# First FFN: later stores of converted chunks and a later first fetch of expert weights; the joint stage's opening in another order

## The chip, the core and the metric

The kernel runs on one core of a Trainium2 chip. The metric is device time in microseconds (us), the median of a few runs of the whole program. The core has a matrix engine (TensorE, PE in the profile), a vector engine (VectorE, DVE), an activation engine (ScalarE, ACT), a general engine (GpSimd, POOL) and a queue engine (SyncE, SP) that here only issues transfers. Each engine takes its instructions strictly in program order: one that waits holds up all that stand behind it on the same engine.

## The reference, cut to what matters

```python
x = attention(q, k, v, n_global, n_local)           # 1536 tokens x 512, 8 heads, local window
h = x @ w_in                                        # first FFN: 512 -> 2048
g = h * np.tanh(softplus(h))
x = g @ w_out                                       # 2048 -> 512
p = domain_probs / (domain_probs.sum(-1, keepdims=True) + 1e-09)
for e in range(4):                                  # second layer: 4 experts, 512 -> 1024 -> 512
    h = np.maximum(x @ w1[e], 0.0)
    out += p[:, e:e + 1] * (h @ w2[e])
```

`attention` and `softplus` stand for code that is left out here. `w_in` and `w_out` arrive as 64-bit floats and are made into 32-bit ones on the chip.

## The kernel before, in words

The 1536 tokens are three blocks of 512. The order of work is: attention of block 0, then the first FFN of block 0 (with the attention of blocks 1 and 2 mixed in at its end), the experts on block 0 (all but the last chunk of weights), the first FFN of blocks 1 and 2, and then a joint stage, in which the experts run on blocks 1 and 2 together. No scheduler reorders anything: each engine's queue is what the code issues, line after line.

**First FFN of block 0** (`first_block`). Its weights come in 16 chunks of 1 MB (64-bit). Four buffers, `big0`, `big1`, `raw0`, `raw1`, take them in turn, so the fetch of chunk c can start only when chunk c-4 has been converted. The string `PLAN` is the order of issue, a letter for each step, counted up as it occurs:

- `a`: ScalarE begins the conversion of a chunk (L602, one instruction, reads the fetched buffer); `t`, three for a chunk: VectorE ends it (L605, L607, L609). The result is the tile `w0`, `w1`, ... in a ring of buffers. After the third `t` of chunk c, `ahead()` issues the fetch that its buffer is free for (L581). In the kernel before, the converted chunk is stored to DRAM (`wfirst`, L613, 512 KB) by the third `t` too, ahead of that fetch. The stores are read again only by the first FFN of block 1.
- `H`: the first product of a chunk, 4 matmuls in plain fp32, which the trace counts as 8 records; `P`: the second product, as long.
- `e`, `c`, `n`, `l`, `u`, `v`, `g`: the gate function between them. `e`, `n`, `l` are ScalarE's (L663, L671, L676 and L677), `c`, `u`, `v`, `g` VectorE's (L667, L682, L686, L690). `g` gives the tile that `P` multiplies.
- `w`: a part of the first expert chunks' split (L629, L632), whose weights `w16`, `w17`, `w18` are fetched in `hidden` (L586) when s reaches a number.

In this stage chunk 4 is, for example, `h4`, `e4`, `n4` and, after `g`, the operand of the fifth `P`.

**The joint stage** (`late_block`) opens with 13 groups of products before it comes to a steady order. `hidden(q, m)` is product m of pair q of expert chunks (L892, 6 matmuls of 128x512): a left operand (`in`, the weights, or `sums`, sums of them) and a right one (`y1`, `y2`, `t2`, `t3`, `t4`: rows of blocks 1 and 2 or their differences), each split into a high and a low half (names that end in h and l). Products 1, 6, 7 and 4 of a pair add up in one PSUM bank (`ha0` for pair 0, `ha1` for pair 1); 2, 5 and 3 use another (`hx0`, `hx1`), each of them starting it anew. Between two of a bank, ScalarE or VectorE has to read the bank (L899, L903): these are the drains. The operands `y2`, `t2`, `t3`, `t4` are made in the generator `combine_rows` from the last FFN's result: subtractions and casts on VectorE and ScalarE, part of them between the products, at each `next(self.combining)`. `project(0)` and `project(1)` (L735, 12 matmuls each) end the FFN of block 2 and the last expert chunk of block 0; the latter is followed by `add_expert`, four VectorE instructions (L796) and the store of the result. `late_part(1, "sums")` is a cast on ScalarE (L873, to `sumsh1`) and two subtractions on GpSimd (L875, to `sumsl1`). `late_project` is L937.

Of the kernel before, what the change touches and what calls it, by code (L numbers as in the profile page):

```python
# [1 line left out]

# [38 lines left out]

PLAN = (
    "SSYXXESYSEXSEDXNXESNTDCTXSENAZNEXATTSCZEDAXANSFSNEXTTDCNEZAXANTETSCZaADXNAtSFNTEXSCTXEAZSEDAVSVaXTTX"
    "CSEZAEADVVFTXTCEZAAaDVVTtTCaAZtAFtHttttHetactntlHteauvgHcetntltaPuavgcetPntltauHvgctntlPteauvgHctntl"
    "tPeuavgctnPtltauvHgtttPecattnltHuvgatPtectnltHtauvgHetcattnHlteuvgPcetntltHwuvgctnPtltieuvHgcwnwlPeu"
    "vgcnljHwjuvgwP12ecnlwHuvg34612Pecnl3uvg5Hw4w6w12Pecnl3uvg54P6Q"
)

# [490 lines left out]
class Body:  # L539
# [48 lines left out]
    def narrow(self, s):  # L588

        if s not in self.w64:
            return
        nc, raw = self.nc, self.w64.pop(s)
        word = raw.bitcast(I32).rearrange("p (n t) -> p n t", t=2)
        top = raw.bitcast(F32).rearrange("p (n t) -> p n t", t=2)[:, :, 1]
        if self.first:

            m = self.w32[s] = self.ring.tile([P, 1024], F32, tag="wl" if s % 2 else "wh", name=f"w{s}")
        else:  # L600
            m = self.w32[s] = self.wpool.tile([P, 1024], F32, tag="w", name=f"w{s}")
        nc.scalar.activation(m, top, AF.Abs, scale=TO_F32)  # L602
        yield
        mi = m.bitcast(I32)
        nc.vector.tensor_scalar(mi, mi, 0x0FFFFFFF, 3, ALU.bitwise_and, ALU.logical_shift_left)  # L605
        yield
        nc.vector.scalar_tensor_tensor(mi, word[:, :, 1], -0x40000000, mi, ALU.bitwise_and, ALU.bitwise_or)  # L607
        yield
        nc.vector.scalar_tensor_tensor(mi, word[:, :, 0], 29, mi, ALU.logical_shift_right, ALU.bitwise_or)  # L609
        if self.first:  # L610

            yield
            nc.sync.dma_start(self.wfirst[s], m)  # L613

    def part(self, s):

# [101 lines left out]
    def project(self, *steps):  # L718

        nc, (kind, t, n) = self.nc, self.steps[steps[0]]  # L720
        opens, closes = steps[0] in self.opens, steps[-1] in self.closes
        if opens:
            acc = [self.acc_ps.tile([P, 512], F32, tag=f"acc{d}", name=f"acc{steps[0]}_{d}") for d in range(4)]
            self.acc = [(d, a, slice(0, 512)) for d, a in enumerate(acc)]
        chunks = [(self.ws.pop(s), self.g.pop(s)) for s in steps]
        for d, acc, h in self.acc:
            for k, ((wh, wl), (gh, gl)) in enumerate(chunks):
                if kind == "ffn":
                    c = slice(512 + d * P, 512 + (d + 1) * P)
                    mms = (wh[:, c], gh), (wl[:, c], gh), (wh[:, c], gl)  # L730
                else:
                    c, w = slice(d * P, (d + 1) * P), slice(512 + h.start, 512 + h.stop)
                    mms = (gh[:, c], wh[:, w]), (gh[:, c], wl[:, w]), (gl[:, c], wh[:, w])
                for m, (a, r) in enumerate(mms):
                    nc.tensor.matmul(acc[:, h], a, r, start=opens and k == 0 and m == 0,  # L735
                                     stop=closes and k == len(chunks) - 1 and m == 2)
            if closes and kind == "moe":
                e = n // NF2
                self.add_expert(t, e, d, acc, h, n == 0 or self.closes[steps[-1]] == 0, self.closes[steps[-1]] == 1)
        if closes and kind == "ffn":  # L740
            self.end_ffn(t)

# [59 lines left out]
    def combine_rows(self):  # L802
# [28 lines left out]
            nc.vector.tensor_tensor(t[2][:, k, :], acc[2 + k], t[1][:, k, :], ALU.subtract)  # L831
        for k in range(2):
            nc.scalar.copy(t[0][:, k, :], acc[2 + k])
        lo(1)
        hi(2)
        yield
        lo(2)
        nc.vector.tensor_tensor(t[3], t[0], t[3], ALU.subtract)
        yield
        hi(3)  # L840
        nc.vector.tensor_tensor(t[4], t[4], t[2], ALU.subtract)
        lo(3)
        hi(0)
        lo(0, nc.gpsimd)
        yield
        hi(4)
        lo(4)
        yield


# [25 lines left out]
        self.wp[q, what] = hi, lo  # L876


    def late_hidden(self, q, m):


        nc = self.nc
        bank, opens, what, at = PRODUCTS[m]
        if opens and m in (1, 2):
            self.hb[q, bank] = self.bank(f"h{bank}{q}")
        ps = self.hb[q, bank]
        (wh, wl), (rh, rl) = self.wp[q, what], self.rows[m]
        n = 0
        for kc in range(2):
            c = slice(at * 256 + kc * P, at * 256 + (kc + 1) * P)  # L890
            for a, r in ((wh, rh), (wl, rh), (wh, rl)):
                nc.tensor.matmul(ps, a[:, c], r[:, kc, :], start=opens and n == 0, stop=n == 5, skip_group_check=True)  # L892
                n += 1
        self.flush()
        if m == 1:
            self.hs[q] = [self.temps[(3 * q + k) % len(self.temps)] for k in range(3)]
        t = self.hs[q]
        if m in (1, 6, 7):
            nc.scalar.copy(t[(1, 6, 7).index(m)], ps)  # L899
        if m in (2, 7, 3):  # L900
            k = {2: 0, 7: 2, 3: 1}[m]
            b = self.hb[q, "x"]
            nc.vector.tensor_tensor(t[k], b, t[k], ALU.add)  # L903
            self.late_relu(q, {2: (0, 0), 7: (1, 1), 3: (1, 0)}[m], t[k])
        if m == 4:
            self.late_relu(q, (0, 1), ps)
# [49 lines left out]
    def late_block(self, project):  # L956


        n, order = NE * NF2 // 2, (1, 2, 6, 5, 7, 4, 3)
        hidden = self.late_hidden  # L960
        hidden(0, 1)
        project(0)
        hidden(0, 2)
        hidden(1, 1)
        next(self.combining)
        hidden(0, 5)
        hidden(0, 6)
        next(self.combining)
        project(1)
        next(self.combining)  # L970
        hidden(0, 7)
        hidden(1, 2)
        self.late_part(1, "sums")
        self.late_weights(1, "out")
        self.late_weights(2, "in")
        hidden(0, 4)
        hidden(0, 3)
        for q in range(1, n + 1):
            tasks = {}
            if q < n:  # L980
# [5 lines left out]
                    tasks[9] = lambda: self.late_part(q + 1, "sums")  # L986
                if q + 2 < n:
                    tasks[8] = lambda: self.late_weights(q + 2, "in")
            left = [m for m in order if q < n and (q > 1 or m > 2)]
            for k in range(8):  # L990
                if k < len(left):
                    hidden(q, left[k])
# [15 lines left out]
    def first_block(self, ready, now):  # L1008
# [46 lines left out]
            return run  # L1055

        def hidden(s):
            if s == 4:
                for c in range(NF1, NF1 + 3):
                    self.fetch(c)  # L1060
            assert n["F"] == 4 and n["t"] >= 3 * s + 3
            self.accumulating = True
            self.hidden_first(s)
            ahead()

        def project(s):
            self.project_first(s)
# [9 lines left out]
        def convert(k):  # L1077
# [1 line left out]
            assert n["a"] > c  # L1079
            next(narrowing[c], None)  # L1080
            ahead()
            if k % 3 == 2:
                next(narrowing[c], None)

        def part(k):
            c, third = divmod(k, 3)
# [35 lines left out]
    def run(self):  # L1122
# [14 lines left out]
                self.closes[s] = 0 if n == NF2 - 1 and kind == "moe" else 1 if s == last - 1 else 2  # L1137
        self.x, self.y, self.outs, self.nr, self.yf, self.rows = {}, {}, {}, {}, {}, {}
        self.w64, self.w32, self.ws, self.h, self.enr, self.g = {}, {}, {}, {}, {}, {}
        self.w2, self.wp, self.late = {}, {}, None  # L1140
        bias = self.bias.rearrange("p h c -> p (h c)")
        self.sums, self.rest = [bias[:, 0:1024], bias[:, 1024:2048]], bias[:, 2048:3072]
        ready = dict(fetch=0, narrow=0, part=0)
# [166 lines left out]
```

## Time and profile before

| | us |
|---|---|
| median of 3 runs | 892.99 (892.88 to 895.15) |
| profiled execution | 892.84 |
| its span | 891.0 |
| TensorE busy in the span | 873.6 (98%), 3848 instructions |
| VectorE, ScalarE, GpSimd busy | 566.5 (64%), 481.8 (54%), 385.9 (43%) |
| granted clock over the span | 0.997 |

A row of a timeline gives the start, the duration, the engine, the line and the tiles of an instruction or of a run of like ones, and in brackets how long the engine had been idle before it and what it waited for. Matmuls are pipelined: the duration of one reaches into the next, so the time that a group costs is read from start to start. A window's row gives, for each engine, its busy time in that stretch and its number of instructions, then the clock that TensorE was granted, the busy share of the 16 DMA engines and their rate.

### The profile page before, as it was taken

The page shows a single profiled execution, that of the slowest core. Times are in us where ns is not written, and L with a number is a line of the kernel's source. Part 1 is how long each engine was busy: PE and PEld are TensorE (multiplying, and loading weights), DVE is VectorE, ACT ScalarE, POOL GpSimd, SP SyncE. Part 2 cuts the span into 40 slices and gives each one's busy share as a digit, 9 for nine tenths or more (in the row PEclk, how much of TensorE's full clock was granted, in tenths as well). Part 3 has the DMA queues.
Part 4 walks back from the last instruction along what each step waited for, and adds up shares of the span by engine and source line. Part 5 has one row for each costly group of instructions (what it writes and reads, how often), then busy time and mean ns, then how long its engine had stood idle before and what let it go on. Part 6 is the DMA issues. An engine that isn't in the chain of part 4 may idle for free.

```text
span 891.0 us, 11253 instructions
## 1 busy us (share of the span) xinstructions
PE 873.6 (98%) x3848; PEld 669.6 (75%) x3848; DVE 566.5 (64%) x1112; ACT 481.8 (54%) x943; POOL 385.9 (43%) x416
## 2 busy tenths in 40 slices
PE   9898999999999999999999999899999999999997
PEld 5543444888888888888888887688888888888886
DVE  6997988766678675566656666445554555555555
ACT  6664556778777766577665566443333333333320
POOL 4000021587868766655310223554444555554420
PEclk9999999999999999999999999999999999999999
DMA  9498533354444441888555640521111111211002
GB/s 326 167 384 303 209 123 104 132 189 143 151 157 147 177 150 48 307 284 294 225 193 199 245 167 0 166 72 47 48 48 48 47 48 51 68 48 48 1 1 98
DMA packets 39858, 126.15 MB, mean 142 GB/s; under 512 B 4080, under 2 KB 6896, under 8 KB 37744
## 3 DMA queue, kind: packets, MB, share of 16 engines
q1 hardware_dynamic: 39648, 125.32, 39.5%
q8 instruction: 32, 0.52, 0.2%
q14 instruction: 34, 0.28, 0.1%
q10 hardware_dynamic: 144, 0.02, 0.0%
HBM read 97.02 MB, written 28.31 MB: 141 GB/s over the span
## 4 chain that ended last, share of the span: by engine, by line
PE 80%; DVE 9%; ACT 4%; DMA 3%; issue 2%; POOL 0%; SPq 0%; DVEq 0%; ACTq 0%; POOLq 0%
PE acc_l L937 20%; PE h L647 19%; PE acc L735 19%; PE ha L892 9%; PE hx L892 7%; DMA big<-in_wff 2%; PE pt L200 2%; PE o L307 2%; DVE w L607 1%; DVE w L609 1%; ACT p L285 1%; DVE nr L686 1%; DVE nr L682 1%; PE acc L783 1%; DMA raw<-in_wff 1%
## 5 line engine op out<-in xcount | busy, mean ns | idle before, releaser
L632 POOL TENSOR_TENSOR wl<-w,wh 128x512 fp32r<-128x512 f32 x90 | 118.8, 1340 | 60.2 <-ACT wh L629 55.1
L796 DVE SCALAR_TENSOR_TENSOR big<-acc_l,prob,big 128x512 f32<-128x512 f32 x120 | 88.7, 746 | 77.9 <-PE acc_l L937 77.8
L875 POOL TENSOR_TENSOR zl<-wout,zh 128x512 fp32r<-128x512 f32 x32 | 40.9, 1298 | 80.7 <-ACT zh L873 80.7
L875 POOL TENSOR_TENSOR sumsl<-bias,sumsh 128x512 fp32r<-128x512 f32 x32 | 41.4, 1316 | 73.1 <-ACT sumsh L873 73.1
L682 DVE SCALAR_TENSOR_TENSOR nr<-e,n 128x512 f32<-128x512 f32 x48 | 33.2, 692 | 53.3 <-ACT n L677 53.3
L899 ACT COPY raw<-ha 128x512 f32<-128x512 f32 x33 | 19.3, 586 | 80.7 <-PE ha L892 80.7
L663 ACT ACTIVATE e<-h 128x512 f32<-128x512 f32 x48 | 28.0, 584 | 60.1 <-PE h L647 25.4
L195 POOL TENSOR_SCALAR p<-p,st 128x256 f32<-128x256 f32 (+1 forms) x58 | 42.0, 736 | 39.9 <-ACT v L249 35.0
L770 PE MATMUL h<-x,w 128*128 128x512 f32 x128 | 56.8, 593 | 0.7 <-ACT x L407 0.7
L735 PE MATMUL acc<-wh,gh 128*128 128x512 f32 x128 | 52.5, 410 | 0.0
L285 ACT ACTIVATE p<-t,st 128x256 f32<-128x256 f32 (+1 forms) x96 | 46.3, 484 | 8.9 <-DVE st L274 8.6
L937 PE MATMUL acc_l<-zh,gh 128*128 128x512 f32 x128 | 50.6, 396 | 0.0
L629 ACT CAST wh<-w 128x1024 fp32r<-128x1024 f32 x48 | 50.2, 1046 | 0.7
L647 PE MATMUL h<-y0h,wh 128*128 128x512 f32 x128 | 50.6, 395 | 0.0
L937 PE MATMUL acc_l<-zh,gl 128*128 128x512 f32 x128 | 50.4, 394 | 0.0
L937 PE MATMUL acc_l<-zl,gh 128*128 128x512 f32 x128 | 50.3, 393 | 0.0
L647 PE MATMUL h<-y0l,wh 128*128 128x512 f32 x128 | 50.3, 393 | 0.0
L735 PE MATMUL acc<-wh,gl 128*128 128x512 f32 x128 | 50.2, 392 | 0.0
L647 PE MATMUL h<-y0h,wl 128*128 128x512 f32 x128 | 50.2, 392 | 0.0
L274 DVE CUSTOM_DVE_ANT_0 t<-s,bias 128x256 f32<-128x256 f32 (+1 forms) x96 | 34.5, 399 | 24.7 <-PE s L261 20.8
L937 PE MATMUL acc_l<-zh,gl_late 128*128 128x512 f32 (+1 forms) x128 | 50.0, 391 | 0.0
L937 PE MATMUL acc_l<-zh,gh_late 128*128 128x512 f32 (+1 forms) x128 | 50.0, 391 | 0.0
(232 smaller groups left out, 2487.7 us busy)
## 6 DMA issues: line engine op xcount, KB each, us to landing
w<-in_wts SPq DMA_DIRECT2D x32, 512.0 KB, 4.6
raw<-in_qkv SPq DMA_DIRECT2D x32, 512.0 KB, 3.6
big<-in_wff SPq DMA_DIRECT2D x8, 1024.0 KB, 7.0
raw<-in_wff SPq DMA_DIRECT2D x8, 1024.0 KB, 7.5
wfirst<-w SPq DMA_DIRECT2D x16, 512.0 KB, 3.2
w<-wfirst SPq DMA_DIRECT2D x16, 512.0 KB, 4.4
wkeep<-wh SPq DMA_DIRECT2D x16, 512.0 KB, 3.5
wkeep<-wl SPq DMA_DIRECT2D x16, 512.0 KB, 2.9
```

What stands on the lines that cost most here:

```text
L195: engine.tensor_scalar(self.p[:, j, 0:self.nk * P], self.p[:, j, 0:self.nk * P], st[:, 2 + j:3 + j], 0.0, ALU.mult, ALU.add)
L285: nc.scalar.activation(p[:, j, 0:n], t[:, j, 0:n], AF.Exp, bias=self.least[:, j:j + 1], scale=-1.0, accum_out=self.sum[:, j:j + 1])
L629: (nc.vector.tensor_copy if copy == "vector" else nc.scalar.copy)(hi, w)
L632: getattr(nc, engine or "gpsimd").tensor_tensor(lo[:, c], w[:, c], hi.bitcast(F32)[:, c], ALU.subtract)
L647: nc.tensor.matmul(ps, a[:, c], r[:, kc, :], start=m == 0, stop=m == 3 * KC - 1)
L682: nc.vector.scalar_tensor_tensor(self.nr[s], e, 1.0, n, ALU.add, ALU.mult)
L735: nc.tensor.matmul(acc[:, h], a, r, start=opens and k == 0 and m == 0, stop=closes and k == len(chunks) - 1 and m == 2)
L770: self.nc.tensor.matmul(ps, self.w32[s][:, kc * P:(kc + 1) * P], self.x0[:, kc, :], start=kc == 0, stop=kc == KC - 1)
L796: nc.vector.scalar_tensor_tensor(o, acc, p, o, ALU.mult, ALU.add)
L875: nc.gpsimd.tensor_tensor(lo[:, c], w[:, c], hi.bitcast(F32)[:, c], ALU.subtract)
L892: nc.tensor.matmul(ps, a[:, c], r[:, kc, :], start=opens and n == 0, stop=n == 5, skip_group_check=True)
L937: nc.tensor.matmul(o, a[:, c], r[:, w], start=n == 0, stop=n == 5)
```

## The change

In the first FFN the store to `wfirst` leaves the conversion and is issued by `hidden(s)`, behind the chunk's first product and behind the fetches that are ready by then. The three fetches of expert weights move from `hidden(4)` to `hidden(10)`. `PLAN` has the same letters in another order: most of the `a` from chunk 4 on stand later, and some `e` do. In the joint stage, product 2 of pair 1 moves up, from behind `project(1)` to in front of product 5 of pair 0; product 6 of pair 1 moves up too; the drains of some products (split off as `late_after`), the cast for `sumsh1` and the steps of `combine_rows` change their places; and the four `add_expert` instructions of `project(1)` are held back, two until after product 7 of pair 0 and two until after the opening.

```diff
@@ PLAN
-    "CSEZAEADVVFTXTCEZAAaDVVTtTCaAZtAFtHttttHetactntlHteauvgHcetntltaPuavgcetPntltauHvgctntlPteauvgHctntl"
+    "CSEZAEADVVFTXTCEZAAaDVVTtTCaAZtAFtHttttHetctntlHtauevgHcattnltPeuvagcetPntltauHvgctntlPteauvgHctntlt"
...
@@ narrow
-        if self.first:
-
-            yield
-            nc.sync.dma_start(self.wfirst[s], m)
@@ project
-                self.add_expert(t, e, d, acc, h, n == 0 or self.closes[steps[-1]] == 0, self.closes[steps[-1]] == 1)
+                add = partial(self.add_expert, t, e, d, acc, h, n == 0 or self.closes[steps[-1]] == 0, self.closes[steps[-1]] == 1)
+                if self.held is None:
+                    add()
+                else:
+                    self.held.append(add)
@@ combine_rows
-        lo(1)
         hi(2)
         yield
+        lo(1)
         lo(2)
+        yield
         nc.vector.tensor_tensor(t[3], t[0], t[3], ALU.subtract)
+        hi(3)
         yield
-        hi(3)
         nc.vector.tensor_tensor(t[4], t[4], t[2], ALU.subtract)
         lo(3)
+        hi(4)
+        lo(4)
         hi(0)
         lo(0, nc.gpsimd)
-        yield
-        hi(4)
-        lo(4)
         yield
@@ late_hidden
-        self.flush()
+        if after:
+            self.flush()
+            self.late_after(q, m)
+
+    def late_after(self, q, m):
+        nc, bank = self.nc, PRODUCTS[m][0]
+        ps = self.hb[q, bank]
         if m == 1:
@@ late_block
-        hidden(1, 1)
-        next(self.combining)
-        hidden(0, 5)
-        hidden(0, 6)
-        next(self.combining)
+        hidden(1, 1, False)
+        combine()
+        self.late_after(1, 1)
+        hidden(1, 2, False)
+        self.late_part(1, "sums")
+        hidden(0, 5, False)
+        combine()
+        hidden(0, 6, False)
+        self.late_after(0, 6)
+        combine()
+        self.held = []
         project(1)
-        next(self.combining)
-        hidden(0, 7)
-        hidden(1, 2)
-        self.late_part(1, "sums")
+        held, self.held = self.held, None
+        hidden(0, 7, False)
+        for run in held[:2]:
+            run()
+        self.late_after(0, 7)
+        hidden(1, 6, False)
+        self.late_after(1, 6)
+        self.flush()
         self.late_weights(1, "out")
         self.late_weights(2, "in")
         hidden(0, 4)
+        self.late_after(1, 2)
         hidden(0, 3)
+        for run in held[2:]:
+            run()
...
-            left = [m for m in order if q < n and (q > 1 or m > 2)]
+            left = [m for m in order if q < n and (q > 1 or m not in (1, 2, 6))]
@@ first_block, hidden(s)
-            if s == 4:
+            if s == 10:
                 for c in range(NF1, NF1 + 3):
                     self.fetch(c)
...
             self.hidden_first(s)
             ahead()
+            self.nc.sync.dma_start(self.wfirst[s], self.w32[s])
@@ first_block, convert(k)
-            if k % 3 == 2:
-                next(narrowing[c], None)
```

SyncE's queue in the first FFN, from the fetch of chunk 8 (into `big0`) on. Before:

```order
L581 DMA big0_124<-in_wff 128x1024
L613 DMA wfirst_166<-w5_643 128x1024
L586 DMA w16_704<-in_wts 128x1024
L586 DMA w17_706<-in_wts 128x1024
L586 DMA w18_708<-in_wts 128x1024
L581 DMA big1_125<-in_wff 128x1024
L613 DMA wfirst_166<-w6_667 128x1024
L581 DMA raw0_122<-in_wff 128x1024
```

The same place now:

```order
L582 DMA big0_124<-in_wff 128x1024
L582 DMA big1_125<-in_wff 128x1024
L1086 DMA wfirst_166<-w4_637 128x1024
L582 DMA raw0_122<-in_wff 128x1024
L1086 DMA wfirst_166<-w5_655 128x1024
L582 DMA raw1_123<-in_wff 128x1024
```

The fetch of chunk 9 (into `big1`) had a store and three fetches of expert weights between it and the fetch of chunk 8, and now has nothing.

ScalarE's queue in the first FFN, where chunk 4's gate meets the conversions of chunks 8 and 9 (`w9<-big1` is the `a` of chunk 9). Before:

```order
L671 ACTIVATE e3_685<-n3_686 128x512
L676 ACTIVATE n3_686<-e3_685 128x512
L677 ACTIVATE n3_686<-n3_686 128x512
L663 ACTIVATE e4_731<-h4_710 128x512
L602 ACTIVATE w9_734<-big1_125 128x1024
L671 ACTIVATE e4_731<-n4_732 128x512
L676 ACTIVATE n4_732<-e4_731 128x512
L677 ACTIVATE n4_732<-n4_732 128x512
L663 ACTIVATE e5_759<-h5_741 128x512
```

The same place now:

```order
L668 ACTIVATE e3_682<-n3_683 128x512
L673 ACTIVATE n3_683<-e3_682 128x512
L674 ACTIVATE n3_683<-n3_683 128x512
L660 ACTIVATE e4_721<-h4_700 128x512
L603 ACTIVATE w8_724<-big0_124 128x1024
L668 ACTIVATE e4_721<-n4_722 128x512
L673 ACTIVATE n4_722<-e4_721 128x512
L674 ACTIVATE n4_722<-n4_722 128x512
L603 ACTIVATE w9_745<-big1_125 128x1024
L660 ACTIVATE e5_753<-h5_731 128x512
```

The conversion of chunk 9 moved from in front of chunk 4's `n` and `l` to behind them; that of chunk 8 moved into its place.

VectorE's queue where the joint stage opens, from the last subtraction on a result of the FFN on. Before:

```order
L831 TENSOR_TENSOR t2_5341<-acc63_3_4659,raw0_122 128x512
L821 TENSOR_TENSOR y2l_5340<-raw0_122,y2h_5339 128x1024
L903 TENSOR_TENSOR bias_89<-hx0_5359,bias_89 128x512
L915 SCALAR_TENSOR_TENSOR gl_late_5311<-bias_89,gh_late_5310 128x512
L821 TENSOR_TENSOR t2l_5343<-t2_5341,t2h_5342 128x1024
L838 TENSOR_TENSOR raw1_123<-raw1_123 128x1024
```

The same place now:

```order
L832 TENSOR_TENSOR t2_5341<-acc63_3_4659,raw0_122 128x512
L910 TENSOR_TENSOR bias_89<-hx0_5358,bias_89 128x512
L822 TENSOR_TENSOR y2l_5340<-raw0_122,y2h_5339 128x1024
L822 TENSOR_TENSOR t2l_5343<-t2_5341,t2h_5342 128x1024
L840 TENSOR_TENSOR raw1_123<-raw1_123 128x1024
L843 TENSOR_TENSOR raw0_122<-raw0_122,t2_5341 128x1024
```

The drain of `hx0` moved in front of `y2l`, and `gl_late` moved out of the way of `t2l`. On TensorE the six matmuls of product 2 of pair 1 (`hx1`) now stand between the last of `ha1` and the first on `y2h`.

## Rows read from the trace of the kernel before

**Rows 1.** Windows: first FFN's stall, joint stage's opening, stretches between and behind.
```profile
72.50:80.50 8.00, 5.42 (x9) 2.22 (x9) 7.16 (x10) 5.25 (x7) 0.00 (x0) 0.79 0.60 243
150.00:540.00 390.00, 389.36 (x1860) 324.06 (x1861) 258.54 (x603) 267.07 (x579) 209.80 (x225) 1.00 0.52 186
542.30:569.80 27.50, 23.31 (x97) 17.69 (x96) 18.55 (x23) 16.70 (x24) 9.69 (x8) 1.00 0.36 115
569.80:885.00 315.20, 315.20 (x1370) 256.85 (x1369) 162.09 (x222) 105.63 (x152) 146.17 (x142) 1.00 0.15 47
```

**Rows 2.** Timeline of TensorE in the first FFN, 69 to 106 us.
```profile
69.15 3.60 PE L783 MATMUL acc<-gl,w 128*128 128x512 f32 x8
75.33 5.40 PE L783 MATMUL acc<-gh,w 128*128 128x512 f32 x8 [2.58 <-DVE gh L690]
...
94.49 10.46 PE L770 MATMUL h<-x,w 128*128 128x512 f32 x24
104.79 1.45 PE L783 MATMUL acc<-gl,w 128*128 128x512 f32 x3
```

**Rows 3.** Timeline of VectorE in the first FFN, 57 to 79 us.
```profile
57.39 1.22 DVE L609 SCALAR_TENSOR_TENSOR w<-big,w 128x1024 int32<-128x1024 int32 x1
...
73.14 0.69 DVE L682 SCALAR_TENSOR_TENSOR nr<-e,n 128x512 f32<-128x512 f32 x1 [2.93 <-ACT n L677]
...
75.20 0.42 DVE L667 TENSOR_SCALAR n<-e 128x512 f32<-128x512 f32 x1
...
78.65 0.69 DVE L682 SCALAR_TENSOR_TENSOR nr<-e,n 128x512 f32<-128x512 f32 x1
```

**Rows 4.** Timeline of ScalarE in the first FFN, 64 to 109 us.
```profile
64.28 0.58 ACT L663 ACTIVATE e<-h 128x512 f32<-128x512 f32 x1
70.13 1.13 ACT L602 ACTIVATE w<-big 128x1024 f32<-128x1024 f32 x1 [5.27 <-DMA big<-in_wff]
...
108.26 1.03 ACT L629 CAST wh<-w 128x1024 fp32r<-128x1024 f32 x1
```

**Rows 5.** Timeline of SyncE's issues around 60 us.
```profile
59.06 1.69 SPq L586 DMA_DIRECT2D w<-in_wts  x3
60.85 0.38 SPq L581 DMA_DIRECT2D big<-in_wff  x1
```

**Rows 6.** DMA issues of 60.8 to 61.2 us: KB, us to landing.
```profile
big<-in_wff SPq DMA_DIRECT2D x1, 1024.0 KB, 9.2
```

**Rows 7.** DMA issues of 84.3 to 84.6 us.
```profile
big<-in_wff SPq DMA_DIRECT2D x1, 1024.0 KB, 5.7
```

**Rows 8.** Window inside the slow second product behind the stall.
```profile
76.00:79.00 3.00, 3.00 (x5) 1.17 (x4) 2.93 (x4) 2.68 (x4) 0.00 (x0) 0.50 0.10 38
```

**Rows 9.** Timeline of TensorE in the joint stage's opening: rows with a wait.
```profile
549.99 0.47 PE L892 MATMUL hx<-y2h,sumsh 128*128 128x512 f32 x1 [0.71 <-DVE bias L903]
...
552.42 0.50 PE L892 MATMUL ha<-t2l,sumsh 128*128 128x512 f32 x1 [0.35 <-DVE t2l L821]
...
560.27 0.50 PE L892 MATMUL ha<-t4l,inh 128*128 128x512 f32 x1 [0.68 <-DVE t4l L821]
...
564.46 0.51 PE L892 MATMUL ha<-t2h,sumsh 128*128 128x512 f32 x1 [1.61 <-ACT sumsh L873]
...
565.82 0.50 PE L892 MATMUL ha<-t2h,sumsl 128*128 128x512 f32 x1 [0.85 <-POOL sumsl L875]
```

**Rows 10.** The chain that ended last, 578 us: steady matmuls without a wait.
```profile
578.28 5.51 PE acc_l L937 x24
```

**Rows 11.** Timeline of VectorE in the joint stage's opening.
```profile
547.61 1.63 DVE L821 TENSOR_TENSOR y2l<-raw,y2h 128x1024 fp32r<-128x1024 f32 x1 [0.31 <-ACT y2h L817]
...
551.15 1.22 DVE L821 TENSOR_TENSOR t2l<-t,t2h 128x1024 fp32r<-128x1024 f32 x1
```

**Rows 12.** Timeline of ScalarE and GpSimd there: a split's cast, a split's subtractions.
```profile
563.38 1.03 ACT L873 CAST sumsh<-bias 128x1024 fp32r<-128x1024 f32 x1
545.60 2.56 POOL L875 TENSOR_TENSOR zl<-wout,zh 128x512 fp32r<-128x512 f32 x2
```

More of the change, by code (lines that the diff above doesn't have):

```diff
@@ L1 @@
 from contextlib import ExitStack
+from functools import partial
 import concourse.bass as bass
@@ L43 @@
     "SSYXXESYSEXSEDXNXESNTDCTXSENAZNEXATTSCZEDAXANSFSNEXTTDCNEZAXANTETSCZaADXNAtSFNTEXSCTXEAZSEDAVSVaXTTX"
-    "CSEZAEADVVFTXTCEZAAaDVVTtTCaAZtAFtHttttHetactntlHteauvgHcetntltaPuavgcetPntltauHvgctntlPteauvgHctntl"
-    "tPeuavgctnPtltauvHgtttPecattnltHuvgatPtectnltHtauvgHetcattnHlteuvgPcetntltHwuvgctnPtltieuvHgcwnwlPeu"
+    "CSEZAEADVVFTXTCEZAAaDVVTtTCaAZtAFtHttttHetctntlHtauevgHcattnltPeuvagcetPntltauHvgctntlPteauvgHctntlt"
+    "aPuevgctnPtltauvHgttatPectntltHauvgtPetctnltHtauvgaHtectntlHteauvgPcetntltHwuvgctnPtltieuvHgcwnwlPeu"
     "vgcnljHwjuvgwP12ecnlwHuvg34612Pecnl3uvg5Hw4w6w12Pecnl3uvg54P6Q"
@@ L876, in late_part, with late_hidden @@
         self.wp[q, what] = hi, lo
-    def late_hidden(self, q, m):
+    def late_hidden(self, q, m, after=True):
         nc = self.nc
@@ L960, in late_block @@
         hidden = self.late_hidden
+        combine = lambda: next(self.combining)
         hidden(0, 1)
@@ L1139, in run @@
         self.w64, self.w32, self.ws, self.h, self.enr, self.g = {}, {}, {}, {}, {}, {}
-        self.w2, self.wp, self.late = {}, {}, None
+        self.w2, self.wp, self.late, self.held = {}, {}, None, None
         bias = self.bias.rearrange("p h c -> p (h c)")
```

## Prediction

> **What bounds the kernel now.** I read the windows first [rows 1]. From 150 to 540 us TensorE is busy for 389.36 of 390 us, from 569.8 to 885 for all of it, at full clock: no change in the order of other engines' work can make these stretches shorter, and nothing in them takes a gain back, since all that feeds them is issued relative to TensorE's progress. Two places are left. In 72.5 to 80.5 TensorE is busy for 5.42 of 8.00 us at a mean clock of 0.79, and in 542.3 to 569.8 for 23.31 of 27.50 us. The reader is to see that the change touches just these two, so the question is how much of each it can win, and whether the wait comes back a little later.
>
> What they lose in all is read from start to start. First FFN: the products follow each other every (104.79 - 94.49) / 3 = 3.43 us where nothing waits. From the fourth second product (69.15) to the one at 104.79 there are nine of them, 30.9 us of work in 35.64 us: 4.74 us lost [rows 2]. Joint opening: the first 96 matmuls of that stage (16 groups of six, from 542.32) run 27.5 us; steady ones take 5.51 / 24 = 0.2296 us [rows 10], so 22.04 us of work and 5.46 us lost. The idle in brackets of its five waits is 0.71 + 0.35 + 0.68 + 1.61 + 0.85 = 4.20 us [rows 9]; the rest is the overlap that a stopped pipeline loses at each of them. Together 10.2 us is the ceiling.
>
> **First FFN: what the stall is.** The timelines, followed backwards, tell one chain. TensorE at 75.33 waits for the gate of chunk 4 [rows 2]. VectorE could not begin it before 73.14, because ScalarE's `l` was late [rows 3]. ScalarE had ended `e` of chunk 4 at 64.86 and then stood until 70.13 at the conversion of chunk 9, whose data were not there, with chunk 4's `n` queued behind it [rows 4]. Those data were fetched at 60.85, behind 1.69 us of issuing three expert fetches [rows 5], and took 9.2 us [rows 6]; a fetch of the same size with less traffic around it took 5.7 [rows 7]. [...]
>
> **What the change does there.** It takes the store and the three expert fetches (1.5 MB) from in front of the fetch of chunk 9, and it puts chunk 4's `n` in front of chunk 9's conversion. I follow VectorE, which has one period of 73.14 to 78.65 = 5.51 us for a chunk: 2.06 for `u`, `v`, `g` and 3.45 for `c` and the three `t` [rows 3]. The conversion of chunk 5 ends at 57.39 + 1.22 = 58.6, which I leave as it is; so the fetch of chunk 9 is issued at 58.6. VectorE then goes on every 5.51 us: gate of chunk 3 from 64.1, of chunk 4 from 69.6, done at 71.7. TensorE comes to that product at 69.15 + 3.43 = 72.6, so it no longer waits, with 0.9 us to spare. Chunk 9's conversion comes after `l` of chunk 4, at about 68.5; its data land between 58.6 + 5.7 = 64.3 and 58.6 + 9.2 = 67.8. Even the slowest fetch seen is hidden.
>
> The next ones in the same way, each fetch issued when VectorE has ended the chunk four before: chunk 10 lands at 69.9 to 73.4, wanted at 74.0; chunk 11 at 75.4 to 78.9, wanted at 75.1, but ScalarE has nothing to do between it and `e` of chunk 6, whose product ends at 79.6, so it may be as late as 78.4; chunk 12 at 80.9 to 84.4, may be as late as 85.3. The tightest place is the gate of chunk 6: product ends 79.6, `e` and `c` 1.0 us, the conversion of chunk 10 3.1, the gate 2.1, which makes 85.9, and TensorE wants it at 86.3. From there VectorE, at 5.51 us a chunk against TensorE's 6.87, runs ahead. I take the whole 4.7; the bounds are 1.8 (the wait shrinks to one that the clock rides out) and 4.74.
>
> **What is moved behind it.** Sixteen stores of 0.5 MB go behind fetches on SyncE; an issue takes some 0.4 us, as the fetch's does [rows 5], and no store waits for more than its converted chunk, so nothing is blocked by them. A store now also holds its ring buffer longer, but the next user comes five buffers later, more than 20 us. The expert fetches now follow the fetch of chunk 15, at about 91; their first use, the cast of `w16`, comes at about 103.5 (108.26 in the trace [rows 4], 4.7 earlier). Each is half a weight fetch, and the slowest of those took 9.2 us: landed by 100.2 and hidden. If late, ScalarE would hold chunk 9's gate, for which TensorE has some 9 us left. The loads of block 1's attention follow the last conversion, which ends 5.9 us earlier than before. Cost: nothing.
>
> **Joint opening: wait by wait.** Product 2 of pair 1 (1.38 us of work whose operands have long been ready) now stands in front of the first product on `y2`. That product waited for the drain of `hx0`, at 549.99, since VectorE did `y2l` first, 1.63 us [rows 9, 11]. With the drain ahead it reads `hx0` at 547.95 to 548.6, and TensorE comes at 550.5: gone, and so is the wait for `t2l` (done at about 551.0, since `gl_late` is out of its way; wanted at 552.3). `project(1)` runs from 553.2 to 556.0. `t4l` no longer follows four `add_expert` instructions: it is done at 556.1 and wanted at 559.1. The two waits for the sums of pair 1 were the largest [rows 9]: the cast began at 563.38, and two such subtractions take 2.56 us [rows 12]. The cast now stands behind the drain of `ha1`, at about 550.5, so that the subtractions end at 554.1, wanted from 557.3. I find no wait left before `late_project`, and the least room at two drains: `hx1` before its product on `y2`, 0.75 us (560.65 against 561.4), and `ha1` before its product on `t4`, 0.35 us. The two `add_expert` instructions held back (1.3 us) sit on VectorE between drains, and their banks are wanted at 568. The gain is 4.2 to 5.5; I take 5.4, since the loss from start to start is what the end sees.
>
> On VectorE and GpSimd one row speaks against this. `y2l` took 1.63 us where `t2l` of the same size took 1.22 [rows 11]; GpSimd's subtractions were under way until 545.60 + 2.56 = 548.16 [rows 12]. The change puts GpSimd's `sumsl1` on top of three such VectorE instructions (two SBUF operands). By the row each of them costs 0.4 more, 1.2 in all, of which the 0.75 of room takes most: 0.5 us of stall.
>
> [...]
>
> **Sum.** 892.84 - 4.7 - 5.4 = 882.7 us for an execution like the profiled one, whose span would be 880.9. It lay 0.15 us under the median of the runs, so I say 882.8.
>
> **Rivals.**
> - *The joint stage keeps a part of its waits.* For it: every drain now hangs on VectorE's chain with under 1 us of room, and GpSimd works beside it. If GpSimd's 2.56 us go wholly into that chain, 1.8 us are lost beyond the room, and a second pair of such subtractions (`y2l` low) may add as much: 884 to 887.
> - *The first FFN's wait comes back one chunk later.* For it: there are still four buffers, so each fetch starts only after a conversion, and one has taken 9.2 us [rows 6]. Against it: 2.1 MB less stand in front. Chunk 11 would have to take over 8.7 us. Then `e` of chunk 6 and the tight gate behind it slip by as much, and if TensorE idles as long as before, its clock falls again: of 4.7 us only 0 to 3 are won: 884.5 to 887.5.
> - *The change does not shorten anything that ends last*, if both happen: 888 to 891.
> - *Slower.* One mechanism could do it: the expert fetches now come 32 us later. If they landed late, ScalarE would stand at the cast of `w16` with the gates of chunks 9 and 10 behind it. TensorE's cover is about 9 us behind 103.5; to use up the 10.1 won as well, they would have to land after 122, 31 us after their issue. Nothing in the profile took that long.
>
> **Chances.** Both stalls gone, 882.2 to 884.0: 0.62. The joint part kept: 0.18. The first FFN's part kept: 0.10. Both: 0.04. Within 0.3% (2.7 us, about what a measurement of this kernel can tell from no change; 890.3 to 895.7): 0.03. Slower: 0.03. Faster by more than that is 0.94. The low end, 881.8, is the ceiling of 10.2 us and the 0.9 us or so by which such readings err; the high end, 887.5, takes in the two partial cases. It leaves out about 1 in 10.
>
> **What would show it.** Right: no bracket on the ScalarE rows of L603 from chunk 8 on, no half clock near 76 us, nine products from the fourth second one in 31 us, the 96 matmuls of the opening in 22 to 22.6 us, the cast of `sumsh1` before that of `t3h`. Wrong: a `DMA big` or `DMA raw` wait of over 1 us on L603 between 64 and 90; matmuls on `y2h`, `t4h` or `hx1` behind a VectorE drain; or VectorE instructions of 128x1024 at 1.6 us and more between 550 and 556, which the range foresees; a change in 150 to 540, where I expect none, would make the whole reading wrong.

## The result and the profile after

The changed kernel takes **882.88 us** (median of 4 runs, 882.74 to 882.95) against 893.29 for the kernel before (4 runs, 892.88 to 895.15). Over all these runs the ratio is 0.9879, 95% interval 0.9862 to 0.9896. The profiled execution took 882.74 us with a span of 880.9, 10.1 us less than the span of before. The prediction was 882.8.

The windows show both places that the change touches. The columns are those of [rows 1]; the last window begins at the same work as the third one there and is as long.

```profile
72.50:80.50 8.00, 8.00 (x20) 3.46 (x19) 7.83 (x10) 4.06 (x6) 0.00 (x0) 1.00 0.75 247
150.00:540.00 390.00, 389.43 (x1874) 326.25 (x1873) 256.48 (x599) 268.62 (x577) 212.81 (x228) 1.00 0.51 182
536.30:563.80 27.50, 26.89 (x115) 21.17 (x114) 22.16 (x25) 18.76 (x27) 14.23 (x10) 1.00 0.29 85
```

In the first FFN the stall and the half clock are gone: TensorE is busy for all of the 8 us at full clock. In the joint opening 0.61 us of idle are left. The stretch between is as before.

TensorE's timeline in the first FFN answers to [rows 2]: no bracket any more.

```profile
68.49 3.60 PE L784 MATMUL acc<-gl,w 128*128 128x512 f32 x8
71.92 3.60 PE L784 MATMUL acc<-gh,w 128*128 128x512 f32 x8
...
89.09 10.46 PE L771 MATMUL h<-x,w 128*128 128x512 f32 x24
99.39 3.60 PE L784 MATMUL acc<-gl,w 128*128 128x512 f32 x8
```

From the fourth second product to the ninth product behind it: 99.39 - 68.49 = 30.90 us, before 35.64. ScalarE's conversions there answer to [rows 4]:

```profile
67.73 1.14 ACT L603 ACTIVATE w<-big 128x1024 f32<-128x1024 f32 x1
73.25 1.15 ACT L603 ACTIVATE w<-raw 128x1024 f32<-128x1024 f32 x1
76.38 1.17 ACT L603 ACTIVATE w<-raw 128x1024 f32<-128x1024 f32 x1 [1.98 <-DMA raw<-in_wff]
82.06 1.17 ACT L603 ACTIVATE w<-big 128x1024 f32<-128x1024 f32 x1
...
91.55 1.14 ACT L603 ACTIVATE w<-raw 128x1024 f32<-128x1024 f32 x1 [1.05 <-DMA raw<-in_wff]
```

Chunk 9 (67.73) does not wait. Chunk 11 (76.38) and chunk 14 (91.55) do, where ScalarE had nothing else to do; no product is late for them.

In the joint opening these are TensorE's rows with a wait (they answer to [rows 9]), then VectorE's (to [rows 11]) and GpSimd's (to [rows 12]).

```profile
554.82 0.50 PE L893 MATMUL hx<-y2h,sumsh 128*128 128x512 f32 x1 [0.19 <-DVE t_late L910]
...
556.81 0.50 PE L893 MATMUL hx<-y2h,sumsh 128*128 128x512 f32 x1 [0.36 <-DVE raw L910]
```

```profile
542.63 1.22 DVE L822 TENSOR_TENSOR y2l<-raw,y2h 128x1024 fp32r<-128x1024 f32 x1
...
546.04 2.34 DVE L843 TENSOR_TENSOR raw<-raw,t 128x1024 f32<-128x1024 f32 x1
548.30 2.33 DVE L822 TENSOR_TENSOR t3l<-raw,t3h 128x1024 fp32r<-128x1024 f32 x1
550.55 2.30 DVE L822 TENSOR_TENSOR t4l<-raw,t4h 128x1024 fp32r<-128x1024 f32 x1
...
554.09 0.68 DVE L910 TENSOR_TENSOR t_late<-hx,t_late 128x512 f32<-128x512 f32 x1
```

```profile
545.55 3.99 POOL L876 TENSOR_TENSOR sumsl<-bias,sumsh 128x512 fp32r<-128x512 f32 x2 [3.39 <-ACT sumsh L874]
550.49 3.52 POOL L825 TENSOR_TENSOR y2l<-raw,y2h 128x512 fp32r<-128x512 f32 x2 [0.94 <-ACT y2h L818]
```

All five old waits are gone; two small ones are left, with a delay of 0.22 us at `t3l` that is too short for a bracket. The 96 matmuls take 23.38 us from start to start (536.32 to 559.70), before 27.50, and 22.04 without any wait. The reader is to see VectorE's three instructions of 2.3 us: each has GpSimd's subtractions beside it (`t3l` for about 1.4 of its 2.33 us, the other two throughout), and the same engine's `y2l`, with GpSimd idle, takes 1.22.

Where the 10.1 us come from, by the two traces: 4.74 in the nine products, 4.12 in the joint opening, 0.66 ahead of the first FFN (its first product starts at 37.49 instead of 38.15), 0.54 at its end (the last second products, 139.45 to 149.82 us, where a wait of 0.27 us for VectorE's `gl` is gone), and under 0.1 in the rest.

### The profile page after: what moved, and what is told of

The parts are those of the page before. It is cut to its first block, busy times and chain, and to the rows that moved or that the text cites. A ratio compares the mean times of both kernels' runs of the same rounds, so it can differ in the third digit from the quotient of the medians.

```text
span 880.9 us, 11248 instructions
## 1 busy us (share of the span) xinstructions
PE 869.7 (99%) x3848; PEld 669.2 (76%) x3848; DVE 569.9 (65%) x1112; ACT 482.3 (55%) x943; POOL 388.6 (44%) x416
## 4 chain that ended last, share of the span: by engine, by line
PE 94%; DVE 2%; DMA 1%; ACT 0%; POOL 0%; issue 0%; ACTq 0%; POOLq 0%; DVEq 0%
PE acc_l L944 20%; PE h L644 20%; PE acc L732 20%; PE ha L893 9%; PE hx L893 7%; PE h L771 6%; PE acc L784 6%; PE pt L201 2%; PE o L308 2%; PE s L262 1%; PE s L261 1%; DMA qk<-in_qk 1%; PE s L365 0%; PE o L403 0%; DVE raw L843 0%; DVE t3l L822 0%
```

## Experiments

Twelve kernels ran, each with profile and 4 to 12 timed runs beside runs of the kernel before. Two lengths are read in every profile, start to start as above: the nine products of the first FFN and the 96 matmuls of the joint opening.

| kernel | median us | nine products | 96 matmuls |
|---|---|---|---|
| before | 893.29 | 35.64 | 27.50 |
| after | 882.88 | 30.90 | 23.38 |
| e1, FFN part alone | 888.50 | 30.90 | 27.54 |
| e2, joint part alone | 887.90 | 34.76 | 23.39 |
| e3, FFN order alone | 888.30 | 30.90 | 28.90 |
| e4, stores and fetches alone | 892.21 | 35.21 | 27.54 |
| e5, before with filler | 892.46 | 34.60 | 29.11 |
| e6, `sumsl` on VectorE | 881.92 | 30.90 | 22.47 |
| e7, `y2l` low too | 883.20 | 30.90 | 23.36 |
| e8, none held back | 883.88 | 30.90 | 24.68 |
| e9, old stores and fetches | 883.12 | 31.51 | 23.37 |
| e10, e1 with filler | 886.98 | 30.90 | 27.56 |
| e11, e1 with early sums | 887.14 | 30.90 | 27.69 |
| e12, e6 with three held | 882.08 | 30.90 | 22.50 |

### The two halves of the change (e1, e2)

e1 is the kernel before with the new PLAN and the fetch and store edits; e2 is the changed kernel with these taken back. The stores go behind a chunk's first product; the expectation of e1 and that of e4 name their place inexactly.

```diff
@@ e1 against before; e2 is after with the same lines taken back
-    "CSEZAEADVVFTXTCEZAAaDVVTtTCaAZtAFtHttttHetactntlHteauvgHcetntltaPuavgcetPntltauHvgctntlPteauvgHctntl"
+    "CSEZAEADVVFTXTCEZAAaDVVTtTCaAZtAFtHttttHetctntlHtauevgHcattnltPeuvagcetPntltauHvgctntlPteauvgHctntlt"
...
-            nc.sync.dma_start(self.wfirst[s], m)
...
-            if s == 4:
+            if s == 10:
...
+            self.nc.sync.dma_start(self.wfirst[s], self.w32[s])
...
```

> All of the change in the first FFN (the order, the stores at the end of a chunk's conversion, the expert fetches at its eleventh product), with the joint opening as before. If the two gains are independent of each other, as the two traces say, TensorE's nine products take 30.9 us instead of 35.64 and the joint opening keeps its 27.5 us for 96 matmuls: 4.7 us from the stall, 0.5 from the end of the first FFN, so about 887.5 to 888.5 us. Rival: the joint opening's gain came from the earlier first FFN after all (more time for VectorE and GpSimd ahead of it); then it is below 886.

> All of the change in the joint opening, with the first FFN as before. By the trace of the changed kernel (96 matmuls in 23.4 us instead of 27.5) it takes 4.1 us off the kernel before: about 889 us, and the stall of 2.6 us and the half clock at 76 us are there unchanged. Rival, the term of the prediction: 5.4 us, about 887.6; it would mean that the 1.3 us lost after the change come from the first FFN's new timing, not from VectorE's and GpSimd's own work at that place.

e1: ratio 0.9946 (0.9929 to 0.9964), 4.8 us. e2: 0.9948 (0.9930 to 0.9965), 4.6 us. The lengths in the table are those of the changed kernel in the one place and of the kernel before in the other: the parts are independent, and e1's rival falls. e2's 96 matmuls take 23.39 us also behind the old first FFN, so the joint gain is 4.1, not 5.4. That the median gives e2 more than 4.1 has a reason of its own, which e10 shows.

e2 also shows the FFN's stall with another clock. TensorE's timeline of e2:

```profile
74.48 3.70 PE L788 MATMUL acc<-gh,w 128*128 128x512 f32 x8 [2.45 <-DVE gh L691]
...
89.35 3.70 PE L788 MATMUL acc<-gh,w 128*128 128x512 f32 x8 [0.87 <-DVE gh L691]
```

Behind a wait of 2.45 us the clock stayed at full (1.00 in each us from 72 to 81; the products take 3.70, not 5.40), and then a second wait of 0.87 us appears, at the gate of chunk 6.

### Order against transfers (e3, e4, e9)

e3 is before with the new PLAN alone, e4 before with the stores and fetches alone, e9 the changed kernel with these two taken back.

```diff
@@ e4 against before (e3 has PLAN's lines of e1 instead); e9 is after with these taken back
-            nc.sync.dma_start(self.wfirst[s], m)
...
-            if s == 4:
+            if s == 10:
...
+            self.nc.sync.dma_start(self.wfirst[s], self.w32[s])
...
```

> The kernel before with the new order of steps in the first FFN alone; stores and expert fetches stay where they were. Theory: the wait came from chunk 4's middle instruction standing behind the conversion of a late chunk on ScalarE; with it in front, the chunk may land as late as before (about 70 us) and TensorE does not wait: 4 us gained or more, 888 to 889 us. Rival: the late data still hold ScalarE, and the gate of chunk 5 or 6 is late instead: under 2 us gained, above 891 us.

> The kernel before with only the stores moved to the end of a chunk's conversion and the expert fetches moved behind the last fetch; the order of the engines' steps stays. Theory: the fetch of chunk 9 starts some 2 us earlier with 2 MB less in front and lands at 65 to 68 us, before or just after ScalarE comes to it, so chunk 4's gate is late by 0.5 us at most and TensorE's clock is not lowered: 4 to 4.7 us gained, 888.3 to 889. Rival: it still lands at 69 or later, TensorE still waits over 1 us there: under 3 us gained, above 890 us.

> The changed kernel with the stores behind each conversion and the expert fetches at the fifth product again, as before; the new order of steps and the whole joint opening stay. Theory (the order alone removes the wait, as the kernel with the order alone said): the same as the changed kernel, 882.7 to 883.1 us. Rival: with the bytes in front, one of the later chunks is late enough in some executions: above 883.5 us.

e3: 0.9942 (0.9924 to 0.9961): the whole gain. ScalarE of e3 still waits for chunk 9:

```profile
69.88 1.15 ACT L602 ACTIVATE w<-big 128x1024 f32<-128x1024 f32 x1 [1.78 <-DMA big<-in_wff]
```

It begins at 69.88, before at 70.13 [rows 4], and TensorE does not wait, since chunk 4's `n` and `l` now stand in front. e4: 0.9990 (0.9976 to 1.0004), no difference that can be told; its theory falls, and the rival's reason with it. Chunk 9 landed early, as expected (its conversion begins at 64.23), and the fifth second product waits no more. Two second products later, ScalarE and TensorE of e4:

```profile
83.27 1.17 ACT L602 ACTIVATE w<-big 128x1024 f32<-128x1024 f32 x1 [3.49 <-DMA big<-in_wff]
```

```profile
88.50 5.25 PE L779 MATMUL acc<-gh,w 128*128 128x512 f32 x8 [2.49 <-DVE gh L686]
```

```profile
89.00:91.00 2.00, 2.00 (x3) 0.68 (x3) 1.97 (x4) 0.59 (x2) 0.00 (x0) 0.50 0.78 313
```

The same stall, with its half clock, has moved to chunk 6: there the old order again has a late conversion in front of the gate. So the order is the cause of the gain. The transfers seem to add a little: e9 ran at 882.74, 882.81, 883.43 and 883.58, and its profile (of the 883.58) has this wait, at the gate that the prediction called the tightest:

```profile
86.65 3.70 PE L788 MATMUL acc<-gh,w 128*128 128x512 f32 x8 [0.34 <-DVE gh L691]
```

The nine products take 0.61 us more than in the changed kernel there. Theory and rival each have a part: two of the four runs are like the changed kernel's (882.74 to 882.95), one is above the rival's 883.5.

### What the low clock costs (e5, e10)

Matmuls that nothing reads fill a wait of TensorE; e5 fills that of the first FFN in the kernel before, e10 the one for `sumsh` in e1.

```diff
@@ e5 against before: PLAN has a y ahead of the fifth P, which calls
+        def fill(k):
+            bank = self.bank(f"fill{k}")
+            for _ in range(3):
+                nc.tensor.matmul(bank, self.ident, self.ident.unsqueeze(1).to_broadcast([P, 4, P]), start=True, stop=True)
@@ e10 against e1
         hidden(0, 3)
+        fill = self.acc_ps.tile([P, 512], F32, tag="acc0", name="fill")
+        for _ in range(2):
+            self.nc.tensor.matmul(fill, self.ident, self.ident.unsqueeze(1).to_broadcast([P, 4, P]), start=True, stop=True)
```

> The kernel before, with three extra matmuls of the identity into a spare bank (computing nothing that is used) in the middle of TensorE's wait of 2.6 us in the first FFN. Theory: 1.8 us of the 4.7 lost there are the granted clock, which falls after the wait; with work in the wait it stays at full, the eight matmuls behind it take 3.6 us instead of 5.4, and the end comes up to 1.8 us earlier: 891 to 892 us at the median. Rival: the clock falls all the same, or another wait takes the gain: 893 us as before. A caution: the kernel with the changed joint opening alone kept full clock behind a wait of 2.45 us, so the fall may not be certain in the kernel before either; the profile decides.

> The kernel with only the first FFN changed, with two extra matmuls of the identity (computing nothing that is used) where TensorE waits for sumsh of pair 1 in the joint opening. Its executions without them lay in two groups, 886.5 to 886.8 and 888.4 to 888.9. Theory: the second group is those in which the granted clock fell to half behind that wait, as in the profile of the kernel with the order alone; with the wait filled no execution falls in it: all at 886.4 to 887.2. Rival: the groups have another cause: both groups again, median 888.4.

e5's timeline of TensorE:

```profile
73.35 2.74 PE L1043 MATMUL fill<-ident 128*128 128x512 f32 x6
75.93 3.60 PE L783 MATMUL acc<-gh,w 128*128 128x512 f32 x8
...
90.69 3.70 PE L783 MATMUL acc<-gh,w 128*128 128x512 f32 x8 [0.86 <-DVE gh L690]
```

The clock stays at full (1.00 in each us from 72 to 81), as the theory said, but the 1.8 us are not won: TensorE comes earlier to chunk 6's gate and waits 0.86 us there, as in e2. The nine products take 1.04 us less, and the median moves by 0.4 (0.9997, 0.9987 to 1.0006), which is not resolved. The half clock thus cost the kernel before about 1 us (0.9 by e2, whose clock stayed up without a filler), not 1.8; the rest would have been a wait.

In the joint opening the clock falls too, in some executions. e3's profile has it, behind the waits for `sumsh` and `sumsl` (1.59 and 0.87 us):

```profile
560.00:563.00 3.00, 2.90 (x7) 2.32 (x8) 1.18 (x2) 0.99 (x2) 1.30 (x2) 0.50 0.82 313
```

e5's profile has it too, in the old opening behind the old first FFN (29.11 us for the 96 matmuls):

```profile
565.00:569.00 4.00, 3.93 (x10) 3.16 (x11) 1.17 (x2) 1.22 (x2) 1.27 (x2) 0.57 0.62 238
```

e1's profile, with waits of 1.62 and 0.86 us there, has not:

```profile
557.00:563.00 6.00, 3.58 (x14) 2.73 (x15) 2.67 (x4) 3.43 (x6) 2.54 (x2) 1.00 0.83 288
```

Its 96 matmuls take 27.54 us against e3's 28.90. The runs of e1 and e3 lie accordingly in two groups, four of twelve at 886.50 to 886.92 and eight at 888.25 to 888.86; the mean clock is 0.998 or 0.999 in each of the four and 0.996 or 0.997 in each of the eight. With the wait filled, all five runs of e10 lie at 886.53 to 887.30; its 96 matmuls take the same 27.56. The second group is the clock. This is why the joint part is worth more in the medians (888.50 to 882.88 = 5.6) than in the profiles (4.1): it takes away a loss that the profile of before happened not to show.

### What is left in the joint opening (e6, e7, e8, e11, e12)

```diff
@@ e6 against after
-        self.late_part(1, "sums")
+        self.late_part(1, "sums", self.nc.vector)
...
@@ e7 against e6
-        lo(0, nc.gpsimd)
+        lo(0)
@@ e8 against after
-        self.held = []
-        held, self.held = self.held, None
+        held = []
@@ e12 against e6
-        for run in held[:2]:
+        for run in held[:1]:
...
-        for run in held[2:]:
+        for run in held[1:]:
@@ e11 against e1
         next(self.combining)
+        self.late_part(1, "sums")
         hidden(0, 5)
...
-        self.late_part(1, "sums")
```

> The changed kernel, with the two subtractions for sumsl of pair 1 on VectorE instead of GpSimd. Theory: VectorE's instructions of 128x1024 took 2.3 us instead of 1.2 because GpSimd subtracted beside them; without it the first two of the three (L843 and t3l) take 1.2 again, minus 2.2 us in VectorE's chain, plus 1.3 for the two it takes over: TensorE's wait for t3l goes, 0.3 to 0.9 us less, 882.0 to 882.6. t4l, beside GpSimd's y2l, stays at 2.3. Rival: those instructions are slow for another reason (TensorE's or the DMA's traffic): they stay at 2.3, VectorE's chain grows by 1.3 us, and the time goes up to 884.

> As the kernel before this one, and the low half of y2 on VectorE too, so that GpSimd does nothing beside VectorE there. Theory: L843, t3l and t4l all take 1.2 us, minus 3.3 us in VectorE's chain against 2.5 for what it takes over: the opening's 96 matmuls in 22.1 to 23.0 us instead of 23.4, 881.6 to 882.6. Rival: the instructions taken over come at the wrong place in VectorE's order and hold back a drain: 883 or more.

> The changed kernel, without holding back two of the four add_expert instructions: all four stand right behind t4l on VectorE. Theory: the drains behind them have no room left since GpSimd's contention took it, so the two held back (1.4 us) come back as a wait of about 1.4 us at the products on y2h: 884 to 884.5. Rival, the prediction's room of 0.35 to 0.75 us still stands: 0.6 to 1 us, 883.5 to 883.9; or they are hidden: 882.9.

> The kernel with only the first FFN changed, and of the joint opening's changes this one alone: the cast of sumsh of pair 1 and GpSimd's two subtractions stand ahead of product 5 of pair 0. Theory: the waits for sumsh (1.62 us) and sumsl (0.86) and the clock that falls behind them go, GpSimd's contention gives some of it back to the waits for VectorE's t3l and t4l: 2 to 2.5 us less than the 886.6 of the undisturbed clock, 884.1 to 884.8. Rival: VectorE, slowed to 2.3 us an instruction, gives it all back: 886 or more.

> The changed kernel with sumsl of pair 1 on VectorE, and three of the four add_expert instructions held back instead of two. Theory: the last wait of the opening, 0.27 us (0.43 from start to start) for VectorE's drain of hx0 before a product on y2h, goes, since VectorE's chain ahead of it is 0.7 us shorter: 0.4 us less than with two held, 881.4 to 881.7. Rival: the drain waits for TensorE's own product, not for VectorE's turn, or the three instructions hold back a later step: 881.9 or more.

**e6** is the fastest kernel: 881.92 us (881.79 to 882.20), 0.96 under after, with 0.91 us less in the 96 matmuls. (Its ratio to before, 0.9880, 0.9865 to 0.9895, cannot tell it from after, since the runs of before scatter by 4 us.) VectorE of e6:

```profile
545.46 1.29 DVE L876 TENSOR_TENSOR sumsl<-bias,sumsh 128x512 fp32r<-128x512 f32 x2 [0.52 <-ACT sumsh L874]
...
547.80 1.22 DVE L843 TENSOR_TENSOR raw<-raw,t 128x1024 f32<-128x1024 f32 x1
549.00 1.22 DVE L822 TENSOR_TENSOR t3l<-raw,t3h 128x1024 fp32r<-128x1024 f32 x1
550.43 1.23 DVE L822 TENSOR_TENSOR t4l<-raw,t4h 128x1024 fp32r<-128x1024 f32 x1 [0.20 <-ACT t4h L818]
```

With GpSimd quiet all three take 1.2, `t4l` too, which now ends as GpSimd's `y2l` begins (551.42). GpSimd was the cause; the rival, that something else slows them, falls.

**e11** looks at it from the other side. The early sums take away the waits for `sumsh` and `sumsl`, the largest of [rows 9], and its five runs (886.39 to 887.25) win nothing against e1's undisturbed ones. GpSimd, VectorE and TensorE of e11:

```profile
546.00 3.78 POOL L871 TENSOR_TENSOR sumsl<-bias,sumsh 128x512 fp32r<-128x512 f32 x2 [3.85 <-ACT sumsh L869]
```

```profile
548.52 2.33 DVE L837 TENSOR_TENSOR raw<-raw,t 128x1024 f32<-128x1024 f32 x1
550.78 2.28 DVE L817 TENSOR_TENSOR t3l<-raw,t3h 128x1024 fp32r<-128x1024 f32 x1
```

```profile
553.12 0.51 PE L888 MATMUL ha<-t3l,sumsh 128*128 128x512 f32 x1 [2.32 <-DVE t3l L817]
...
553.97 0.63 PE L888 MATMUL ha<-t3l,sumsh 128*128 128x512 f32 x1
...
557.34 0.39 PE L888 MATMUL ha<-t4h,inl 128*128 128x512 f32 x1
```

Its theory falls, and the rival holds by its number (886 or more), but VectorE's slow instructions are only one part of the reason. They turn the waits of 1.62 and 0.86 us into one of 2.32 for `t3l`. Behind it the clock falls: its mean over 536.3 to 563.8 us is 0.94 (1.00 in the changed kernel), and the eight matmuls from 553.97 to 557.34 take 3.37 us instead of 8 x 0.23 = 1.84. So some 1.5 of the 27.69 us of this profile are the clock, and without it, by this estimate, the early sums would have won about 1.4 us against e1's 27.54. Whether the clock fell in its other runs is not known. In the changed kernel, with the same slow instructions, TensorE loses 0.22 us at `t3l`: there the new order of products and drains leaves room for them.

**e7** gives e6's gain back: `y2l` low on VectorE (1.22 us) stands in front of the drain `t_late`, and TensorE waits 0.51 and 0.36 us at the products on `y2h`: its theory falls, its rival holds. **e8**: 1.3 us more in the opening, 1.0 in the median, which lies just below the theory's 884 and in the rival's range. What decides for the theory is the row: the wait for `t_late` grows from 0.19 to 1.53 us, by as much as the two instructions take (2.72 us for four), so no room is left there. TensorE of e8:

```profile
556.15 0.50 PE L893 MATMUL hx<-y2h,sumsh 128*128 128x512 f32 x1 [1.53 <-DVE t_late L910]
```

**e12** wins nothing: 882.08 (881.99 to 882.12), in the rival's range. GpSimd and VectorE of e12:

```profile
551.52 2.65 POOL L825 TENSOR_TENSOR y2l<-raw,y2h 128x512 fp32r<-128x512 f32 x2 [9.33 <-ACT y2h L818]
```

```profile
552.33 0.68 DVE L910 TENSOR_TENSOR t_late<-hx,t_late 128x512 f32<-128x512 f32 x1
552.93 1.79 DVE L922 SCALAR_TENSOR_TENSOR gl_late<-bias,gh_late 128x512 fp32r<-128x512 f32 x1
```

The `gl_late` moved 0.56 us earlier, into the time of GpSimd's `y2l`, and took 1.79 us instead of e6's 1.12. Neither theory nor rival gave this reason: GpSimd's work takes the gain.

## Why the prediction was right, point by point

- **The bound, and that nothing in the steady stretches changes:** right; 389.43 of 390 us busy.
- **First FFN, -4.7:** right to the size (4.74), with the times of the steps: chunk 9's conversion at 67.73 (predicted 68.5), chunk 11's data at 76.38 (75.4 to 78.9), the product on chunk 6's gate at 85.66 (wanted at 86.3), 0.4 us behind the gate's end, as predicted. (The prediction's terms for that gate add up to 85.8, not 85.9; this changes nothing.) Of the two edits named there, the order alone is enough (e3), and the transfers alone move the stall to chunk 6 (e4). The account that chunk 9's earlier landing matters was not needed: the rival "the wait comes back one chunk later" would have come true had the order stayed. The lower bound of 1.8 us, which is what the half clock cost the eight matmuls by [rows 2] (5.40 - 3.60), was too high: with the clock at 1.00 there, e5's nine products take 1.04 us less and e2's 0.88, so that about 0.8 of the 1.8 became a wait.
- **Stores and expert fetches, 0:** right as a cost; the cast of `w16` begins at 101.94 us and waits for nothing. Moving the two may give a little, 0.6 us in one profile (e9); the prediction did not say how the 4.7 divide between them and the order.
- **Joint opening, -5.4:** this term was mis-sized; it measured 4.12. The mechanism was right: the cast of `sumsh` stands at 544.42, ahead of that of `t3h` at 546.15, and the five waits are gone. Two steps failed. The stall of 0.5 us that the prediction works out from the row never reached the term: 5.46 less 0.5 is 5.0, and the sum took 5.4. And "by the row each of them costs 0.4 more" was too low a price: the `y2l` of [rows 11] had met only the last 0.55 us of GpSimd's work, while the three in the changed kernel lost 1.08 to 1.12 us each (2.34, 2.33 and 2.30 against 1.22), 3.3 in all, and 1.34 us of stall remain. `t3l` lost as much as the others with GpSimd beside it for only 1.4 us, and GpSimd's two pairs grew as well, to 3.99 and 3.52 us from 2.56 [rows 12] and 2.65 (e10). How the two engines hold each other up is not shown. The 1.8 us of the prediction's first rival (2.56 less the room of 0.75) was nearer than the 0.5 from the row, in part by luck: its 2.56 us are less than the 3.3 measured, and the room of 0.75 us is less than the 2.0 or so that stayed hidden (3.3 - 1.34).
- **The sum was right by luck, because stretches that it did not name made up for this term:** 0.66 us ahead of the first FFN and 0.54 at its end. The first is not shown to be the change's: in the profiles of before, after and e1 to e9 the first product starts anywhere from 37.42 to 38.15, and e3, e4 and e5, whose steps up to there are those of before, start at 37.68 to 37.77. The second stretch took 10.37 us in after, e1, e3 and e4, 10.44 in e5, 10.70 in e2 and 10.91 before; what decides it was not tried.
- **The base:** the sum stood against one execution with one fall of the clock. Over all timed runs the kernel before lies at 890.65 to 895.17 us, with mean clocks from 0.999 down to 0.993; that the number of falls in the two places makes this spread fits e3, e5 and e10, but no profile of its other runs shows it. The changed kernel lies within 0.21 us. The prediction did not see that the joint opening's waits risk the clock as well (0.50 in e3's profile, 0.57 in e5's).
- **Its own signs:** the time lies where it put "both stalls gone", but a quarter of the joint opening's loss stayed (1.34 of 5.46 us). Of its signs of being right, three came (full clock near 76 us, 30.90 us for the nine products, the cast of `sumsh1` ahead of that of `t3h`) and two did not: L603 has brackets, and the 96 matmuls took 23.38 us, not 22 to 22.6. Of its four signs of being wrong, three came: the 1.98 us for `raw` on L603, products on `y2h` behind drains, and VectorE's 2.3 us (from 546 us on, since all of it came earlier). The one on L603 was badly chosen, for the prediction itself let chunk 11 land as late as 78.4 without harm. The other two point at the term that failed.

## What to carry to other kernels

An instruction that waits for data should stand behind everything on its engine that the bottleneck needs next: bringing the data earlier only moved the stall (e4, 2.49 us at chunk 6), putting the wait last removed it (e3, nine products in 30.90 us). Before a subtraction is moved to GpSimd, or next to one, look at what VectorE does beside it: its subtractions of 128x1024 took 2.30 to 2.34 us there instead of 1.22, and the subtraction was cheaper on VectorE itself once (e6, 881.92 us) and not the second time (e7, 883.20). Taking away a wait that may cost the clock was worth more in the medians (5.6 us for the joint part) than in profiles that happened to keep the clock (4.1).

## What the hardware did that was not expected

- VectorE's instructions were not all slowed by GpSimd. In e10 four `add_expert` instructions, which take one operand from PSUM, ran beside the whole of GpSimd's `y2l` at 0.68 us each (in e7, with GpSimd idle, two took 1.41), and GpSimd's two took 2.65 in all. GpSimd and VectorE of e10:

```profile
550.53 2.65 POOL L820 TENSOR_TENSOR y2l<-raw,y2h 128x512 fp32r<-128x512 f32 x2 [8.07 <-ACT y2h L813]
```

```profile
550.67 2.72 DVE L792 SCALAR_TENSOR_TENSOR big<-acc,prob,big 128x512 f32<-128x512 f32 x4
```

- The length of a wait did not decide whether the clock fell: after 2.58 us it fell to 0.50 (before) [rows 8], after 2.49 too (e4), after 2.32 it fell as well (e11, a mean of 0.94 over 536.3 to 563.8 us), but after 2.45 it stayed at 1.00 (e2); after 1.59 and 0.87 it fell to 0.50 (e3), after 1.62 and 0.86 it stayed at 1.00 (e1). What else decides it stays open here.
